# Retention and two expert layers: the first loads, the gate weights and the place of the early ranks rearranged

## The chip, the cores and the metric

The kernel runs on one core of a Trainium2 chip. The metric is the device time of one execution in microseconds; three executions of the kernel before were timed. A core has five engines with a queue of instructions each: TensorE (PE) multiplies matrices, VectorE (DVE), ScalarE (ACT) and GpSimd (POOL) work on tiles, and SyncE (SP) issues transfers (DMA). ACT and POOL issue some transfers too.

## The reference, cut to what matters

Three layers follow each other. q, k and v are (2, 8, 768, 64): two batches, eight heads, 768 tokens, 64 columns.

```python
Dmask = np.where(rel >= 0, lam[:, None, None] ** rel[None, :, :], 0.0)
...
intra = np.einsum('bhic,bhjc->bhij', qb, kb) * Dmask[None]
intra = np.einsum('bhij,bhjd->bhid', intra, vb)
inter = np.einsum('bhid,bhde->bhie', qb * lam_pow[None], kv_state)
...
kv_state = lam_block[None, :, None, None] * kv_state + np.einsum('bhsd,bhse->bhde', kb_dec, vb)
```

That is the retention. Its output, 1536 tokens of 512 columns, goes through a first layer of 8 experts, two for each token, chosen by logits with noise:

```python
logits = x @ w_gate
noise_scale = np.log1p(np.exp(x @ w_noise))
noisy_logits = logits + noise_scale * noise
top2 = np.argpartition(-noisy_logits, 2, axis=1)[:, :2]
...
h = np.maximum(x[mask] @ w1[e], 0.0)
out[mask] += top2_w[mask, k, None] * (h @ w2[e])
```

A second layer of 8 experts takes one expert for each token (`np.argmax(logits, axis=1)`) and has gate weights of its own.

## The kernel before, in words

The retention runs over 12 tiles of 128 tokens, j = 0 to 11, six for each batch. A tile has these pieces on PE, with the copies that other engines make behind them:

- `front(j)`: the transposes of k (L599, four products into the bank `hp`, which ACT copies to `kT` at L601), and for every second tile those of q for two tiles at once (L576, ACT copies to `qT` at L579). The rows of q come from memory with two tokens in turn; `q_rows` sorts them by a copy to `qp` (L558 and L563) ahead of the transposes. L584 makes `qd`, q times the powers of lam.
- `scores(j)` (L632): eight products of k and q into two banks `tr`; DVE multiplies each bank by the mask `dm` to `at` (`masked`, L637).
- `rows(j - 1)` (L700): the products of the tile before with `iw`, a tile that holds the gate weights of the first layer and its noise weights, an identity, and the gate weights of the second layer. DVE takes the logits (L711, L712) and ACT the rows (L709).
- `mix(j)`: the products of `qd` with the state (L679) and of v with `at` (L688), copied by ACT to `xT` (L692), then `state(j)` (L657, bank `yp3`), which DVE adds to the state `st` (L664).

Products of fp32 operands take two passes, so that a product which the program names once stands twice in the trace. The tile framework orders the instructions by their priority and by explicit edges (`tc.issue_after`, here mostly through `behind("name")`, which holds a piece behind the last instruction that `turn` has under that name); each engine then goes through its queue in that order.

At the start nothing can be done before the first loads. SP's queue issues them in the order lam, k of tile 0, two halves of q of tiles 0 and 1, v of tile 0, k of tile 1, q of tiles 2 and 3, v of tile 1, and then the gate and noise weights straight into `iw` and, later, the noise to `nz`: each of these is cut in runs of 32 bytes, because 8 neighbouring numbers belong to one partition. Meanwhile PE multiplies zeros (`unread`, L179): two such products, then the product that spreads lam over the partitions (L185), then five more, and three more between the transposes of k and those of q. Their results are not read.

Among the tiles, expert weights are fetched (`fetch`, tiles `wst`, on SP's queue) in turns that a table of j sets, and rounded by ACT (L108). The first expert is given its tokens early, from the first nine tiles. At j = TA = 9 DVE works out which tokens chose it (`first_marked`, `mbA`); at j = 10 PE counts them (`ranks_of`, L319 and L322, nine products into the bank `yp3`, which `state(9)` used before), DVE turns the counts into numbers `cA` (L763), marks slots with them (`marks`, L381), PE multiplies the marks with the token numbers (`one_hot`, L403), DVE copies the result (L405, `tabi`), PE turns it (L408), DVE makes indices (L409 to L413, `Asrc`) and POOL gathers the rows with them (L530, tiles `xg`). The transposes of these rows (L884) are the last of the retention's part on PE; behind them come the experts (L920 to L922).

## Time and profile before

| | |
|---|---|
| three runs | 594.77, 597.16, 597.49 us; median 597.16 us |
| profiled execution | 595.33 us, of which 593.7 us are the span of the trace |
| PE busy | 583.0 us, 98% of the span |
| DVE, ACT, POOL busy | 375.9, 279.4 and 182.5 us |
| clock of PE, mean over the span | 0.998 of full speed |

The rows further down come from this one profiled execution. A row of the timeline has the start and length of a run of equal instructions in microseconds, counted from the start of the span, then engine, line, operation, out<-in, shapes, and the number of instructions; in brackets stands how long the engine was idle before it and what released it.

### The profile page before, as it was taken

To read this page: it belongs to the slowest core of one execution; us is meant where nothing else is said; L and a number is where in the kernel's file an instruction comes from. 1 tells how busy PE (TensorE), PEld (TensorE's weight loads), DVE (VectorE), ACT (ScalarE), POOL (GpSimd) and SP (SyncE) were. 2 spreads that over 40 slices of the span, in tenths; PEclk is the share of its full clock that TensorE was granted. 3 is DMA by queue.
4 is the path that set the end of the run, shared out by engine and by line. 5 is a ranking of instruction groups with operands and counts; after the bars stand their busy time and mean duration, and the time that the engine had idled before them with its cause. 6 is when DMAs were issued, how large, how long until landed. Compare 5 with 4: busy or idle time off the path is not lost. (4 is left out here: it accounts for less than half of the span.)

```text
span 593.7 us, 11601 instructions
## 1 busy us (share of the span) xinstructions
PE 583.0 (98%) x4305; PEld 554.5 (93%) x4305; DVE 375.9 (63%) x859; ACT 279.4 (47%) x488; POOL 182.5 (31%) x254
## 2 busy tenths in 40 slices
PE   9999999999999999999999999999999999999996
PEld 8988898989999999999999999898889999998996
DVE  5579789765464454543635555447888568667893
ACT  4666431464344433533534434146137367467782
POOL 4976300606041050040220502033175334231204
PEclk9999999999999999999999999999999999999999
DMA  9899505349345377375443621381389967966741
GB/s 183 221 288 279 182 35 195 104 146 357 132 136 172 103 245 224 86 249 177 164 159 106 214 72 54 73 283 69 105 276 340 335 217 236 324 208 198 265 147 36
DMA packets 104868, 109.76 MB, mean 185 GB/s; under 512 B 35699, under 2 KB 80755, under 8 KB 104802
## 3 DMA queue, kind: packets, MB, share of 16 engines
q1 hardware_dynamic: 96722, 83.05, 46.2%
q0 software_dynamic: 8080, 25.88, 12.5%
q8 instruction: 36, 0.59, 0.5%
q14 instruction: 30, 0.25, 0.1%
HBM read 91.89 MB, written 18.71 MB: 186 GB/s over the span
## 5 line engine op out<-in xcount | busy, mean ns | idle before, releaser
L114 DVE TENSOR_TENSOR wl<-wst,wh 128x1024 fp32r<-128x1024 f32 x107 | 133.5, 1256 | 51.9 <-ACT wh L108 49.6
L108 ACT CAST wh<-wst 128x1024 fp32r<-128x1024 f32 x107 | 111.5, 1048 | 35.0 <-PE yp L921 25.3
L920 PE MATMUL hp<-x,wh 128*128 128x364 f32 (+9 forms) x352 | 116.0, 330 | 0.5 <-ACTq L1520 0.5
L921 PE MATMUL hp<-x,wh 128*128 128x364 f32 (+9 forms) x352 | 115.6, 329 | 0.0
L922 PE MATMUL hp<-x,wl 128*128 128x364 f32 (+9 forms) x352 | 114.9, 327 | 0.0
L1008 ACT ACTIVATE h<-hp 128x364 fp32r<-128x364 f32 (+9 forms) x88 | 41.2, 468 | 154.3 <-PE hp L922 147.5
L922 PE MATMUL yp<-h,wl 128*128 128x364 f32 (+8 forms) x320 | 105.9, 331 | 0.0
L920 PE MATMUL yp<-h,wh 128*128 128x364 f32 (+8 forms) x320 | 105.6, 332 | 0.0
L921 PE MATMUL yp<-h,wh 128*128 128x364 f32 (+8 forms) x320 | 105.4, 330 | 0.2 <-DVE h L1009 0.2
L1009 DVE SCALAR_TENSOR_TENSOR h<-hp,h 128x364 fp32r<-128x364 f32 (+9 forms) x88 | 46.3, 526 | 59.5 <-ACT h L1008 59.1
L1167 POOL DMA_INDIRECT x<-y,Rdst x25 | 24.7, 988 | 176.8 <-DVE y L1141 174.7
L920 PEld LDWEIGHTS hp<-x,wh 128*128 128x128 f32 x352 | 66.1, 188 | 1.5 <-ACTq L1520 0.8
L921 PEld LDWEIGHTS hp<-x,wh 128*128 128x128 f32 x352 | 66.1, 188 | 0.5
L922 PEld LDWEIGHTS hp<-x,wl 128*128 128x128 f32 x352 | 66.1, 188 | 0.0
L921 PEld LDWEIGHTS yp<-h,wh 128*128 128x128 f32 x320 | 60.3, 188 | 1.0 <-DVE h L1009 0.6
L922 PEld LDWEIGHTS yp<-h,wl 128*128 128x128 f32 x320 | 60.3, 188 | 0.0
L920 PEld LDWEIGHTS yp<-h,wh 128*128 128x128 f32 x320 | 59.9, 188 | 0.0
L912 DVE TENSOR_TENSOR x<-tr,x 128x128 fp32r<-128x128 f32 (+11 forms) x68 | 27.3, 434 | 26.3 <-ACT x L911 25.7
L911 ACT CAST x<-tr 128x128 fp32r<-128x128 f32 (+11 forms) x68 | 24.4, 386 | 33.4 <-PE tr L910 32.8
L541 POOL TENSOR_TENSOR xg<-xg 128x512 f32<-128x512 f32 (+1 forms) x16 | 24.0, 1502 | 42.6 <-DMA xg<-x,Tsrc 27.8
L530 POOL DMA_INDIRECT xg<-x,Rsrc x25 | 28.7, 1150 | 18.9 <-DVE slt L500 11.6
L1132 PE MATMUL tr<-iw,yT 128*128 128x136 f32 (+3 forms) x224 | 34.2, 287 | 0.1
(393 smaller groups left out, 1041.7 us busy)
## 6 DMA issues: line engine op xcount, KB each, us to landing
wst<-in_moe_w_dram SPq DMA_DIRECT2D x107, 512.0 KB, 4.9
more<-in_moe_w_dram SPq DMA_DIRECT2D x21, 512.0 KB, 5.3
ldk<-in_k_dram SPq DMA_DIRECT2D x12, 256.0 KB, 5.4
ldv<-in_v_dram SPq DMA_DIRECT2D x12, 256.0 KB, 5.8
out_dram<-zero SPq DMA_DIRECT2D x12, 256.0 KB, 4.9
x<-xr SPq DMA_DIRECT2D x11, 256.0 KB, 4.8
ldq<-in_q_dram SPq DMA_DIRECT2D x5, 512.0 KB, 5.8
ldq<-in_q_dram SPq DMA_DIRECT2D x2, 256.0 KB, 4.0
```

The lines of the kernel that those rows point to most:

```text
L108: tail["cast"] = nc.scalar.copy(hi, st).ins
L114: tail["low"] = nc.vector.tensor_sub(lo, st, hi.bitcast(F32)).ins
L530: i = nc.gpsimd.indirect_dma_start(out=r, out_offset=None, in_=x, in_offset=bass.IndirectOffsetOnAxis(ap=src(s)[:m], axis=0))
L911: a = nc.scalar.copy(hi[:, d, :n], ps[:, :n])
L912: v_ = nc.vector.tensor_sub(lo[:, d, :n], ps[:, :n], hi[:, d, :n].bitcast(F32))
L920: nc.tensor.matmul(ps, a[0], b[0], start=start, stop=False)
L921: nc.tensor.matmul(ps, a[0], b[1], start=False, stop=False)
L922: tail["pe"] = nc.tensor.matmul(ps, a[1], b[0], start=False, stop=stop).ins
L1008: tail["act"] = nc.scalar.activation(hh, ps, AF.Relu).ins
L1009: tail["dve"] = nc.vector.scalar_tensor_tensor(hl, ps, 0.0, hh.bitcast(F32), op0=OP.max, op1=OP.subtract).ins
L1132: nc.tensor.matmul(ps[:m, i, :], self.yT[:, 2 * b + i, s * r:s * r + m], iw[:, 2 * b + i, gates2], start=True, stop=True)
L1167: i = nc.gpsimd.indirect_dma_start(out=target, out_offset=bass.IndirectOffsetOnAxis(ap=dst, axis=0), in_=y, in_offset=None, bounds_check=t ...
```

## The change

The first loads come in another order and shape. lam goes to ACT's queue. q of tiles 0 and 1 is loaded as two tiles in its natural order, 256 KB each, so its sorting copies go; `first_front_q` transposes four blocks of it per tile and makes one copy. SP's order is now k, q, v of tile 0, then k, q, v of tile 1. Of the products of zeros, 2 + 3 + 1 are left of 2 + 5 + 3. The gate weights, noise weights and noise are loaded as 24 rows of 4 KB (`load_whole`) on ACT's queue behind the copy of q; eight transposes on PE (`gate_weights`, L230 in the new file) turn them behind `mix(0)`, and four copies on DVE bring them to `iw` and `nz`. Each fetch of expert weights at j = 2 to 6 moves to j = 1 to 5. At j = 10 the ranks stand between the two halves of the scores, both masks stand behind the marks, the product with the marks stands ahead of `front_k(11)`, and the second half of `qd` (L854 on DVE before) is made by POOL. The diff, cut (left out: the new place of a q load in `load`, names that edges refer to, and two edges that put a copy behind another):

```diff
-        parts = (slice(0, HP), slice(HP, H)) if not j else (slice(0, H),)
-        return [lambda h=h: nc.sync.dma_start(t[:, h].rearrange("p h r d -> p h (r d)"), a[:, h]) for h in parts]
+        nc.sync.dma_start(t.rearrange("p h r d -> p h (r d)"), a)
+
+    def first_q():
+        t = ldp.tile([P, H, 2, D], F32, name="ldq", bufs=2).rearrange("p h r d -> p (h r d)")
+        for j in range(2):
+            qkv["q", j] = t[:, j * H * D:(j + 1) * H * D].rearrange("p (h d) -> p h d", h=H)
+        return [lambda j=j: nc.sync.dma_start(qkv["q", j], q[0, :, j * P:(j + 1) * P, :].rearrange("h p d -> p h d"))
+                for j in range(2)]
...
-    i = nc.sync.dma_start(lam1, lam.rearrange("(o h) -> o h", o=1))
+    i = nc.scalar.dma_start(lam1, lam.rearrange("(o h) -> o h", o=1))
+    whole = rt.tile([P, 2, ROW], F32, name="xg", bufs=4).rearrange("p a b -> p (a b)")[:3 * DC + NT, :P * E]
     with tc.issue_after(i.ins):
-        rows_of("k", k, 0)
-        for part in load_q(0):
-            part()
-        written = rows_of("v", v, 0).ins
+        nc.scalar.preload_act_table_set("natural_log_exp_and_others")
+    rows_of("k", k, 0)
+    q_parts = first_q()
+    q_parts[0]()
+    rows_of("v", v, 0)
+    rows_of("k", k, 1)
+    q_parts[1]()
+    written = rows_of("v", v, 1).ins
...
-        unread(5)
+        unread(3)
...
-    with tc.issue_after(written):
-        rows_of("k", k, 1)
-        load_q(2)[0]()
-        rows_of("v", v, 1)
-        nc.sync.dma_start(iw[:, :, :E], g1.rearrange("(c p) e -> p c e", p=P))
-        nc.sync.dma_start(iw[:, :, E:G], gn.rearrange("(c p) e -> p c e", p=P))
...
+    def load_whole():
+        for g, src in enumerate((g1, gn, g2)):
+            nc.scalar.dma_start(whole[g * DC:(g + 1) * DC], src.rearrange("(c p) e -> c (p e)", p=P))
+        nc.scalar.dma_start(whole[3 * DC:], noise.rearrange("(t p) e -> t (p e)", p=P))
+
+    def gate_weights():
+        ps = bank("yp2", [P, E, 3 * DC + NT])
+        n = 3 * DC + NT
+        for e in range(E):
+            turn["state"] = nc.tensor.transpose(ps[:, e, :], whole.rearrange("t (p e) -> t e p", e=E)[:, e, :],
+                                                ident[:n, :n]).ins
+        with tc.issue_after(turn["at"]):
+            for g, a in enumerate((0, E, G + P)):
+                nc.vector.tensor_copy(iw[:, :, a:a + E], ps[:, :, g * DC:(g + 1) * DC].rearrange("p e c -> p c e"))
+            nc.vector.tensor_copy(nz, ps[:, :, 3 * DC:].rearrange("p e t -> p t e"))
...
+    def first_front_q(j):
+        if not j:
+            QT[0] = aw.tile([P, HP, 2, P], F32, name="qT")
+            QD[0] = aw.tile([P, HP, 2, P], F32, name="qd")
+        ps = bank("hp", [P, HP, P])
+        for hp in range(HP):
+            turn["front"] = nc.tensor.transpose(ps[:, hp, :], pair(qkv["q", j], hp), ident).ins
+        turn["copied"] = nc.scalar.copy(QT[0][:, :, j, :], ps).ins
         if j:
-            t = qkv["q", j + 1] = aw.tile([P, 2, H, D], F32, name="qp", bufs=1)
-            with behind("xT", "copied"):
-                nc.scalar.copy(t.rearrange("p r h d -> p h r d"), qkv["q", j])
-            return
-        t = qkv["q", 1] = aw.tile([P, 2, H, D], F32, name="qp", bufs=1)
-        for x, hs in ((nc.scalar.copy, slice(0, HP)), (nc.vector.tensor_copy, slice(HP, H))):
-            with tc.issue_after(decays):
-                i = x(t[:, :, hs].rearrange("p r h d -> p h r d"), qkv["q", 0][:, hs])
-        with tc.issue_after(i.ins):
-            powers_of_q()
+            nc.gpsimd.tensor_mul(QD[0][:, :, 1, :], QT[0][:, :, 1, :], pq)
+
+    def apart(i):
+        tc.add_manual_dep(i.ins, turn["marked"].name, mybir.DependencyInfo(
+            mybir.DependencyClass.Sync, mybir.DependencyReason.DATA), reason="behind the marks")
+        turn["pool"] = i.ins
...
+            with tc.issue_after(decays):
+                powers_of_q()
+        with behind("rows" if j > 1 else "front"):
+            if j < 2:
+                first_front_q(j)
+            elif j % 2 == 0:
+                front_q(j)
+        if not j:
+            with behind("copied"):
+                load_whole()
             with behind("front"):
-                unread(3)
-            q_rows(0)
-        with behind("rows" if j > 1 else "state" if j else "front"):
-            if j % 2 == 0:
-                front_q(j)
+                unread(1)
...
+            if hp == 2 and j == TA + 1:
+                with tc.high_priority(offset=300), tc.issue_after(i.ins):
+                    first_ranked(s1, "yp3")
+                    turn["marked"] = marks(ohA, cA, EARLY[0], range(T0, TA))
+                turn["state"] = tail["ranks"]
             for s in range(2):
                 r = slice(s * D, s * D + D)
                 with behind("state"):
                     i = nc.tensor.matmul(ps[s][:, hp, :], KT[j][r, hp, :], qt[r, hp, j % 2, :], start=True, stop=True)
         turn["scores"] = i.ins
-
-        def masked(s):
-            AT[j, s] = aw.tile([P, HP, P], F32, name="at", bufs=3)
-            turn["at"] = nc.vector.tensor_mul(AT[j, s], ps[s], dm[:, s::2, :]).ins
-
-        masked(0)
+        with behind("marked") if j == TA + 1 else ExitStack():
+            for s in range(2):
+                AT[j, s] = aw.tile([P, HP, P], F32, name="at", bufs=3)
+                turn["at"] = nc.vector.tensor_mul(AT[j, s], ps[s], dm[:, s::2, :]).ins
         if j == TA + 1:
-            with tc.high_priority(offset=300), behind("scores"):
-                first_ranked(s1, "yp3")
-                i = marks(ohA, cA, EARLY[0], range(T0, TA))
-            with tc.issue_after(i):
-                masked(1)
-        else:
-            masked(1)
+            apart(nc.gpsimd.tensor_mul(QD[j - j % 2][:, :, 1, :], QT[j - j % 2][:, :, 1, :], pq))
...
-                if j == 0:
-                    nc.sync.dma_start(iw[:, :, G + P:], g2.rearrange("(c p) e -> p c e", p=P))
-                    nc.sync.dma_start(nz, noise.rearrange("(t p) e -> p t e", p=P))
...
+        if j == TA + 1:
+            with tc.high_priority(offset=300), behind("rows"):
+                selA = one_hot("A", cA, aux1, *EARLY, True, "yp3", oh=ohA)
+                gA = gather(selA[0], EARLY[0], EARLY[0] // EARLY[1], x1[:TA * P, :])
+                turn["picked"] = selA[-1]
+            turn["rows"] = turn["chosen"]
         if not j:
             turn["state"] = turn["scores"]
             state(0)
             front(1)
             mix(j)
+            with behind("state"):
+                gate_weights()
         elif j + 1 < NT:
             front(j + 1)
-        if j == TA + 1:
-            with tc.high_priority(offset=300), behind("front"):
-                selA = one_hot("A", cA, aux1, *EARLY, True, "yp3", oh=ohA)
-                gA = gather(selA[0], EARLY[0], EARLY[0] // EARLY[1], x1[:TA * P, :])
-                turn["picked"] = selA[-1]
-            with tc.high_priority(offset=200), behind("line"):
-                nc.vector.tensor_mul(QD[j - j % 2][:, :, 1, :], QT[j - j % 2][:, :, 1, :], pq)
...
-                for _ in range({2: 1, 3: 1, 4: 1, 5: 1, 6: 1, 9: 1, 10: 2}.get(j, 0)):
+                for _ in range({1: 1, 2: 1, 3: 1, 4: 1, 5: 1, 9: 1, 10: 2}.get(j, 0)):
```

The instructions at the places that this moves stand as follows. First comes PE's queue from its start: `yp` with a number is the bank that takes a product, `zero` the tile of zeros, `xg` the tile with lam (and, in the new kernel, the one with the whole gate weights). Before:

```order
L179 MATMUL yp_118<-zero 128x128 x2
L185 MATMUL yp_121<-xg 128x8
L179 MATMUL yp_124<-zero 128x128 x5
L599 MATMUL hp<-iw,ldk 128x128 x4
L179 MATMUL yp_199<-zero 128x128 x3
L576 MATMUL hp<-iw,qp 128x128 x8
L632 MATMUL tr<-qT,kT 128x128 x8
L657 MATMUL yp_248<-ldv,kd 64x64 x8
L599 MATMUL hp<-iw,ldk 128x128 x4
L688 MATMUL yp_269<-at,ldv 64x128 x8
L632 MATMUL tr<-qT,kT 128x128 x8
```

The same stretch in the changed kernel:

```order
L191 MATMUL yp_123<-zero 128x128 x2
L197 MATMUL yp_126<-xg 128x8
L191 MATMUL yp_129<-zero 128x128 x3
L626 MATMUL hp<-iw,ldk 128x128 x4
L588 MATMUL hp<-iw,ldq 128x128 x4
L191 MATMUL yp_212<-zero 128x128
L670 MATMUL tr<-qT,kT 128x128 x8
L687 MATMUL yp_234<-ldv,kd 64x64 x8
L626 MATMUL hp<-iw,ldk 128x128 x4
L588 MATMUL hp<-iw,ldq 128x128 x4
L719 MATMUL yp_262<-at,ldv 64x128 x8
L230 MATMUL yp_273<-iw,xg 128x24 x8
```

The transposes of q have been split, four ahead of the first scores and four behind the second k, and eight products of 24 columns stand ahead of the second scores, which follow as the next row. ACT's queue from its start, before:

```order
L153 ACT_TABLE_LOAD
L563 COPY qp<-ldq 128x4x2x64
L601 COPY kT<-hp 128x512
L579 COPY qT<-hp 128x512 x2
L601 COPY kT<-hp 128x512
L692 COPY xT<-yp_269 128x512
```

And in the changed kernel:

```order
L164 DMA xg<-in_lam_dram 1x8
L167 ACT_TABLE_LOAD
L628 COPY kT<-hp 128x512
L589 COPY qT<-hp 128x4x128
L223 DMA xg<-in_moe_w_gate_dram 4x1024
L223 DMA xg<-in_moe_w_noise_dram 4x1024
L223 DMA xg<-in_moe_w_gate_dram 4x1024
L224 DMA xg<-in_moe_noise_dram 12x1024
L628 COPY kT<-hp 128x512
L589 COPY qT<-hp 128x4x128
L723 COPY xT<-yp_262 128x512
```

Five issues of transfers have come into ACT's queue, four of them between the first copy of q and the copies for tile 1. DVE's queue at j = 10, from the sum of `state(9)` to the copy of the transposed choice, before:

```order
L664 TENSOR_TENSOR st_172<-st_172,yp_1108 64x4x64 x2
L637 TENSOR_TENSOR at<-tr,dm 128x512
L763 SCALAR_TENSOR_TENSOR cA<-yp_1133,mbA 128x4
L765 TENSOR_SCALAR doneA<-yp_1133 128x1
L381 TENSOR_SCALAR oh<-slot_152,cA 128x288 x4
L637 TENSOR_TENSOR at<-tr,dm 128x512
L711 TENSOR_REDUCE lgs<-yp_1154 128x16
L711 TENSOR_REDUCE lt<-yp_1159 128x16
L712 TENSOR_TENSOR lgs<-lgs,lt 128x16
L405 COPY tabi<-yp_1179 2x288
L854 TENSOR_TENSOR qd<-qT,pq 128x4x128
L409 COPY Aoa<-yp_1190 96x3x2
```

And in the changed kernel:

```order
L694 TENSOR_TENSOR st_167<-st_167,yp_1114 64x4x64 x2
L796 SCALAR_TENSOR_TENSOR cA<-yp_1133,mbA 128x4
L798 TENSOR_SCALAR doneA<-yp_1133 128x1
L403 TENSOR_SCALAR oh<-slot_147,cA 128x288 x4
L675 TENSOR_TENSOR at<-tr,dm 128x512 x2
L743 TENSOR_REDUCE lgs<-yp_1161 128x16
L743 TENSOR_REDUCE lt<-yp_1166 128x16
L745 TENSOR_TENSOR lgs<-lgs,lt 128x16
L428 COPY tabi<-yp_1179 2x288
L432 COPY Aoa<-yp_1190 96x3x2
```

Both masks now stand behind the marks, and the product for `qd` is gone from this queue. On PE, three of the four products of state and `qd` (L679) stood ahead of L408 before; in the changed kernel one does.

## Rows read from the trace of the kernel before

**Rows 1.** The page: busy us, share of the span and instructions of each engine.

```profile
PE 583.0 (98%) x4305; PEld 554.5 (93%) x4305; DVE 375.9 (63%) x859; ACT 279.4 (47%) x488; POOL 182.5 (31%) x254
```

**Rows 2.** Waits of PE, 8 to 76 us: us in total, times, longest us.

```profile
PE tr L884 <- DMA xg<-x,Asrc: 0.7, 1, 0.7
PE yp L700 <- ACT xT L692: 0.4, 1, 0.4
PE hp L599 <- DMA ldk<-in_k_dram: 0.4, 1, 0.4
```

**Rows 3.** Timeline of PE, 1 to 14 us.

```profile
1.19 1.22 PE L179 MATMUL yp<-zero 128*128 128x128 f32 x4 [1.19 <-POOL zero L169]
2.35 0.59 PE L185 MATMUL yp<-xg 1*128 1x8 f32 x2
2.87 2.50 PE L179 MATMUL yp<-zero 128*128 128x128 f32 x10
5.16 1.06 PE L599 MATMUL hp<-iw,ldk 128*128 128x128 f32 x4
...
7.30 1.11 PE L576 MATMUL hp<-iw,qp 128*128 128x128 f32 x8
8.65 1.20 PE L632 MATMUL tr<-qT,kT 64*128 64x128 f32 x16 [0.24 <-ACT qT L579]
...
10.40 0.66 PE L599 MATMUL hp<-iw,ldk 128*128 128x128 f32 x4
...
12.24 1.16 PE L632 MATMUL tr<-qT,kT 64*128 64x128 f32 x16
```

**Rows 4.** Timeline of SP's queue, 0.9 to 5 us, and of ACT, 7 to 9.5 us.

```profile
0.94 0.36 SPq L157 DMA_DIRECT2D xg<-in_lam_dram  x1
1.36 0.41 SPq L134 DMA_DIRECT2D ldk<-in_k_dram  x1
...
2.98 0.51 SPq L134 DMA_DIRECT2D ldv<-in_v_dram  x1
3.53 0.99 SPq L134 DMA_DIRECT2D ldk<-in_k_dram  x1
...
8.01 1.07 ACT L579 COPY qT<-hp 128x512 f32<-128x512 f32 x2 [1.16 <-PE hp L576]
```

**Rows 5.** Transfers issued near 1.4, 3, 3.6 and 9 us: KB, us to landing.

```profile
ldk<-in_k_dram SPq DMA_DIRECT2D x1, 256.0 KB, 3.3
...
ldv<-in_v_dram SPq DMA_DIRECT2D x1, 256.0 KB, 4.9
...
ldk<-in_k_dram SPq DMA_DIRECT2D x1, 256.0 KB, 5.4
...
iw<-in_moe_w_noise_dram SPq DMA_DIRECT2D x1, 16.0 KB, 4.3
```

**Rows 6.** Timeline of DVE, PE and POOL, 62 to 76 us.

```profile
62.80 0.85 DVE L664 TENSOR_TENSOR st<-st,yp 64x256 f32<-64x256 f32 x2
63.71 0.18 PE L319 MATMUL yp<-mbA,tri 128*128 128x5 bf16 x1
64.61 1.46 DVE L381 TENSOR_SCALAR oh<-slot,cA 128x288 bf16<-128x288 f16 x4
65.98 0.68 DVE L637 TENSOR_TENSOR at<-tr,dm 128x512 f32<-128x512 f32 x1
66.77 0.94 PE L679 MATMUL yp<-qd,st 128*128 128x128 f32 x6
66.98 0.44 DVE L405 COPY tabi<-yp 2x288 f32<-2x288 f32 x1
68.83 1.16 POOL L530 DMA_INDIRECT xg<-x,Asrc  x1 [3.47 <-DVE Asrc L413]
70.96 1.29 DVE L637 TENSOR_TENSOR at<-tr,dm 128x512 f32<-128x512 f32 x2 [0.15 <-PE tr L632]
```

**Rows 7.** Timeline of ACT, 33 to 37 us.

```profile
34.32 1.05 ACT L108 CAST wh<-wst 128x1024 fp32r<-128x1024 f32 x1 [1.61 <-DMA wst<-in_moe_w_dram]
```

More of the change, by code (lines that the diff above doesn't have):

```diff
@@ L321, in ranks_of @@
             o = max(0, t + 1 - sl.start)
[L322 to L323 removed]
+            tail["ranks"] = nc.tensor.matmul(ps[:, o:, :], ones, mb[:, t:t + 1, :].to_broadcast([P, n + 1 - o, e]),
+                                             start=False, stop=(t == sl.stop - 1)).ins
         return ps
@@ L585, in half @@
                     if "marked" in turn:
-                        tc.add_manual_dep(i.ins, turn["marked"].name, mybir.DependencyInfo(
-                            mybir.DependencyClass.Sync, mybir.DependencyReason.DATA), reason="behind the marks")
+                        apart(i)
         half(0)
-        if j:
-            turn["half"] = lambda: half(1)
-        else:
-            half(1)
+        turn["half"] = lambda: half(1)
     def front_k(j):
@@ L669, in state @@
             if c + 1 < NC - 1:
-                turn["pool"] = nc.gpsimd.tensor_mul(st[c % 2], new, dec.to_broadcast([P, HP, P])).ins
+                with behind("pool") if "marked" in turn else ExitStack():
+                    turn["pool"] = nc.gpsimd.tensor_mul(st[c % 2], new, dec.to_broadcast([P, HP, P])).ins
     def mix(j):
```

18 lines of the change are left out of this document (11 added, 7 removed).

## The prediction, made before the changed kernel ran

> **What bounds the kernel now.** First the page's table of engines: TensorE (PE) is busy for 98% of the span [rows 1], so time can only be won where PE waits or does work that nobody needs. Next, the waits of PE in the stretch that the change touches, 8 to 76 us: three count, 0.7 us for the last gathered rows, 0.4 us for a copy of ScalarE (ACT), 0.4 us for a load of k [rows 2]. From 76 us on PE runs one expert after the other, and the diff touches nothing there: what the first 76 us gain or lose moves everything behind them, and nothing else does. Then the timeline from the start. The reader is to see two things in it. Four products of 128 columns take 1.06 us at 5.16 and 0.66 us at 10.40, and eight from 7.30 on take 1.11 us [rows 3]: until about 7.4 us PE runs at the lower of its two levels (1.2 GHz), after that at 2.4 GHz, and it had worked almost without a gap since 1.19 us [rows 3] when the clock rose. And the scores of tile 0 start at 8.65 right behind two copies of ACT [rows 3, 4]: the start is a chain of load, transposes, copy. Last the timeline from 62 to 76 us, where the early choice of tokens is made, from the ranks (L319) by marks (L381), product and copy (L405) to the gather (L530) for which PE waits at its end [rows 2, 6].
>
> **The start.** lam leaves SP's queue, so k's first load is issued at 0.94 and not at 1.36 [rows 4] and lands 0.42 us earlier. It landed at 1.36 + 3.3 = 4.66 [rows 4, 5], so now at about 4.24. The loads behind it are q, v, k, q, v, of 256 KB each. v of tile 0 landed at 2.98 + 4.9 = 7.9 and the k behind it at 3.53 + 5.4 = 8.9 [rows 4, 5], a step of 1.05 us for 256 KB. So q lands at 5.3, v at 6.35, k of tile 1 at 7.4, its q at 8.45, its v at 9.5. The rows of q need no sorting copy any more: four transposes at the low clock (1.06) end at 6.4, one copy on ACT (two half ones took 1.07 [rows 4]; I take 0.6) ends at 7.0, and the scores start at about 7.1, 1.55 us before the old 8.65. The products of zeros that go (four of ten) stood only in front of these waits and win nothing themselves.
>
> Then the gain is given back. From scores 0 to scores 1 it took 12.24 - 8.65 = 3.59 us [rows 3]. Into this stretch come four transposes of tile 1's q, of which the pitch is 0.11 (1.11 for eight behind each other [rows 3], with the tail), so 0.45, and eight transposes of the gate weights with 24 columns each. These have no row; from below they cost nothing, from above the 1.11 of eight with 128 columns; I take 0.6, and 0.15 for one more change of operands. Without a wait scores 1 would start at 7.1 + 3.6 + 0.45 + 0.75 = 11.9, 0.35 us earlier than before.
>
> But they wait for the noise, and that is the last of four loads that ACT issues. By the order of its waits it takes the semaphore of tile 1's v, so ACT stands still until that v has landed at 9.5. Behind it on ACT's queue stand the copies of k and q of tile 1 (ready at about 10.8 to 11.4 then, early enough for scores 1). How long the noise takes from 9.55 on is the disputed price. From below: lam, four bytes a head and with nothing else under way, went from its issue at 0.94 to the product at 2.35 that read it [rows 3, 4], 1.4 us. From above: the 16 KB of noise weights took 4.3 us behind the big loads in SP's queue [rows 5]. I take 2.2, nearer to lam, because the new loads are 24 runs of 4 KB on a queue of their own, where the old ones were 3072 runs of 32 bytes. Landed at 11.75; PE would have been there at 7.1 + 3.6 + 0.45 = 11.15. So PE waits 0.6 us and scores 1 start at 12.5, **0.25 us later** than before; by the lower bound 0.35 earlier, by the upper one 2.35 later. The four copies to the tiles that hold weights and noise lie on VectorE (DVE) under scores 1 (1.16 us [rows 3]) and cost nothing; without that cover some 0.7 us.
>
> The Trainium skill bears on that price: DMA: Bandwidth & Descriptors, section "Queues, rings and completion order", says that each DMA engine takes turns between the queues it has work for, packet by packet. By it a load on ACT's queue does not stand behind SP's backlog, and the start would come out 0.35 us earlier instead of 0.25 later. No row of before has two queues of loads at work, so the trace neither shows nor denies it; it is the first rival.
>
> **The loop between.** Every fetch of expert weights moves one turn forward (j = 1 to 5 instead of 2 to 6), and the 3072 short runs are gone from in front of k and v. ACT waited 1.61 us for a weight tile before its cast at 34.32 [rows 7], the copy behind it came late, and PE waited the 0.4 us. The k load that PE missed by 0.4 us stood behind weights in the queue. With an earlier fetch and a freer queue both waits should go: **-0.8**, at worst 0 (one fetch more now stands ahead of that k: 512 KB, by the step above 2.1 us, against the gains just named). What is late next is the gather.
>
> **The ranks inside the scores.** At j = 10 the ranks stand between the halves of the scores. They need the bank that state 9 has just left, and DVE reads that bank until 62.80 + 0.85 = 63.65; the ranks already started right there, at 63.71 [rows 6]. So they cannot come earlier; the second half of the scores, which PE did meanwhile, comes behind them: 0.6 later, half of the 1.16 that scores take [rows 3]. On DVE both masks now follow the marks, which end at 64.61 + 1.46 = 66.07. Two masks take 1.29 (row at 70.96), and from the end of the one mask (65.98 + 0.68) to L405 at 66.98 it took another 0.32 for three small ones [rows 6]. So L405 starts at 66.07 + 1.29 + 0.32 = 67.7 instead of 66.98, or at 67.6 with the overlap that follows from their pitch: 0.6 later, and L408 and the gather behind it with it. QD's product (L854) goes from DVE to GpSimd (POOL) and lies there ahead of the gather; POOL had been idle for 3.47 us before it [rows 6], so it costs nothing; without that gap it would cost at least the 0.68 that DVE takes for a mask of that size [rows 6]. On PE two of the L679 products that stood ahead of L408 (six passes in 0.94) now stand behind it, four passes of 0.11, so PE comes to the gathered rows 0.6 + 0.45 = 1.05 late. It waited 0.7 for them. Gather 0.6 late: **+0.6**; were the rows there in time, 1.05 - 0.7 = +0.35; and were the wait of 0.7 a thing of this one execution, +1.05.
>
> **Sum.** +0.25 - 0.8 + 0.6 = +0.05 us on the profiled execution's 595.33 (span 593.7 and 1.63 around it): 595.4. The median of the three runs is 597.16, 1.8 us above the profiled one, and the runs lie 2.7 apart, about 0.5%; less than that a measurement of this kernel can hardly tell from no change. On the median I say **597.2**.
>
> **Rivals.** *The loads of ACT pass the backlog* and the gather comes in time: -0.35 - 0.8 + 0.35 = -0.8, so 596.4. For it: small runs, own queue. Against: ACT itself is held until 9.5. Chance 0.25. *The same with more:* the queue so relieved that waits too small for the list of waits go too. From scores 1 on PE's row has small gaps only, so I allow 2 us more, 594.4 or below; chance 0.1. *The clock rises later*, the one on the slower side. Fewer products of zeros leave PE idle ahead of k at 4.2, ahead of q at 5.2, ahead of the scores at 6.9 and ahead of the gate weights, where before it worked without a gap up to the rise at 7.4. A microsecond more at the low level costs half a microsecond of work (1.06 against 0.66 and less [rows 3]). If it rises only behind the gate weights, near 13, that is (13 - 7.4) / 2 = 2.8 us, so 600.0; it decides against the forecast from a rise near 9 on. The Trainium skill speaks for this rival: TensorE: Matmul & The Clock Gate, Part 1, has the throttled state as the default, which activity releases. Chance 0.2. *The change does nothing at j = 10:* the ranks wait for DVE anyway, which is counted above.
>
> **How the numbers follow.** Forecast 0.45, loads that pass 0.25, much relieved queue 0.1, late clock 0.2. The first two lie between 596.4 and 597.5 and, with the bounds of the noise (-0.6 to +2.1) and of the gather (-0.25 to +0.45) and the scatter of the runs, between 595 and 599. The range reaches to both others: 594.3 to 600.0. Faster by over 0.5% (below 594.2) only in a part of the relieved queue: 0.1. Slower by over 0.5% (above 600.1) in the worse part of the late clock and with a noise that lands as late as the upper bound: 0.1. Same: 0.8.
>
> **What the profile after would show.** The first scores near 7.1 and PE idle ahead of the transposes with 24 columns, released by a DMA: right on the start; no idle time there and scores 1 before 12: the first rival. Groups of four at 1.06 us behind 7.5 us: the late clock. No wait for wst or ldk in ACT's and PE's rows: right on the loop. The ranks released by DVE's sum, L405's successor 0.6 us later against the ranks, and PE still waiting for the gather: right at j = 10. The forecast is wrong if the stretch up to the first expert product has become more than 3 us longer or shorter, or if PE loses or wins behind it.

## The result: 1% slower, and the profile after

The changed kernel takes 602.38 us (median of 6 runs, 601.49 to 603.51), the kernel before 596.77 us (6 runs, 594.77 to 597.49): 1.0096 times as long, 95% interval 1.0077 to 1.0116. Forecast was 597.2 us, with a range up to 600.0, and a chance of 0.1 for slower by over 0.5%. The profiled execution took 602.59 us with a span of 601.0 us, against 593.7 before.

First the table of engines on the page of the changed kernel, and PE's waits from 8 to 85 us (us in total, times, longest):

```profile
PE 587.7 (98%) x4305; PEld 558.2 (93%) x4305; DVE 372.9 (62%) x861; ACT 278.8 (46%) x487; POOL 184.6 (31%) x254
```

```profile
PE yp L230 <- DMA xg<-in_moe_noise_dram: 3.0, 1, 3.0
PE yp L341 <- DVE st L694: 0.4, 1, 0.4
PE yp L719 <- DVE at L675: 0.2, 1, 0.2
```

PE's share is the same as in [rows 1], but it is busy 4.7 us longer with equally many instructions: some of its work has become slower. The three waits of [rows 2] are gone, and one new wait is longer than the three together. The timeline of PE shows both, and answers to [rows 3]:

```profile
2.87 1.65 PE L191 MATMUL yp<-zero 128*128 128x128 f32 x6
4.35 1.09 PE L626 MATMUL hp<-iw,ldk 128*128 128x128 f32 x4
5.44 1.11 PE L588 MATMUL hp<-iw,ldq 128*128 128x128 f32 x4
...
7.23 2.08 PE L670 MATMUL tr<-qT,kT 64*128 64x128 f32 x16 [0.25 <-ACT qT L589]
...
10.29 1.12 PE L626 MATMUL hp<-iw,ldk 128*128 128x128 f32 x4
11.20 0.86 PE L588 MATMUL hp<-iw,ldq 128*128 128x128 f32 x4
11.99 1.09 PE L719 MATMUL yp<-at,ldv 128*64 128x128 f32 x16
16.10 1.04 PE L230 MATMUL yp<-iw,xg 24*128 24x24 f32 x8 [3.01 <-DMA xg<-in_moe_noise_dram]
17.07 2.08 PE L670 MATMUL tr<-qT,kT 64*128 64x128 f32 x16
19.08 2.29 PE L731 MATMUL yp<-iw,xT 128*128 128x144 f32 x8
...
25.34 1.16 PE L670 MATMUL tr<-qT,kT 64*128 64x128 f32 x16
```

The last row is the scores of tile 2. In the kernel before it stood at 18.20:

```profile
18.20 1.16 PE L632 MATMUL tr<-qT,kT 64*128 64x128 f32 x16
```

The reader is to see the same pieces with two lengths. Scores (L670) take 2.08 us at 7.23 and at 17.07 and took 1.16 to 1.20 before; L719 at 11.99 takes 1.09, the length at the upper level. By the record of the granted clock it rises to 2.4 GHz at 11.73 (before: 7.44), falls to 1.2 GHz at 15.14, 2.1 us into the wait for the noise (13.09 to 16.10), and rises again at 21.97. Two stretches of the changed kernel in one view (us, then busy us and instructions of PE, PEld, DVE, ACT and POOL, the clock, the DMA share and GB/s):

```profile
11.73:15.14 3.41, 1.36 (x19) 0.94 (x17) 0.00 (x0) 2.52 (x4) 3.11 (x8) 1.00 1.28 236
15.14:21.97 6.83, 5.87 (x36) 5.62 (x37) 2.20 (x8) 0.74 (x2) 1.77 (x8) 0.50 1.05 238
```

PE works 5.87 us at half speed in the second one. The queue of ACT, 6 to 13 us, says why the noise is late, and the rows of SP's queue stand below it:

```profile
6.59 0.58 ACT L589 COPY qT<-hp 128x512 f32<-128x512 f32 x1 [0.53 <-PE hp L588]
6.60 0.25 ACTq L223 DMA_DIRECT2D xg<-in_moe_w_gate_dram  x1
6.89 0.31 ACTq L223 DMA_DIRECT2D xg<-in_moe_w_noise_dram  x1
8.03 0.26 ACTq L223 DMA_DIRECT2D xg<-in_moe_w_gate_dram  x1
10.52 0.30 ACTq L224 DMA_DIRECT2D xg<-in_moe_noise_dram  x1
11.45 0.58 ACT L628 COPY kT<-hp 128x512 f32<-128x512 f32 x1 [4.27 <-PE hp L626]
```

```profile
5.12 1.33 SPq L134 DMA_DIRECT2D ldv<-in_v_dram  x1
6.50 1.15 SPq L134 DMA_DIRECT2D ldk<-in_k_dram  x1
7.68 1.14 SPq L143 DMA_DIRECT2D ldq<-in_q_dram  x1
8.87 1.23 SPq L134 DMA_DIRECT2D ldv<-in_v_dram  x1
10.28 1.69 SPq L134 DMA_DIRECT2D ldk<-in_k_dram  x1
```

The noise is issued at 10.52, when v of tile 1 (issued at 5.12) has landed at 10.50: ACT held it back until then, because both loads use one semaphore. By its semaphore the noise lands at 15.96, 5.4 us behind its issue, and PE goes on at 16.10. Of these 5.4 us, 2.9 pass before its first packet moves (13.42), 1.4 while its 48 KB move (to 14.82) and 1.1 from there to the semaphore. Ahead of it SP had issued k, q and v of tile 2 (256, 512 and 256 KB). With the loads of tiles 0 and 1 that makes 2560 KB, and 2478 KB of SP's queue had moved at 13.42. The first loads of gate weights show the same: issued from 6.60 on, when SP had issued the 1536 KB of tiles 0 and 1, they begin to move at 9.20, when SP's queue has moved 1527 KB.

Measured from scores to scores in the two profiles, the loss sits in one place. Scores of tile 2 start at 25.34 instead of 18.20: **+7.1**. From there to scores of tile 10 it takes 43.0 instead of 44.4: **-1.4**. From scores 10 (68.34; 62.62 before) to the first expert product (83.98; 76.89 before) 15.6 instead of 14.3: **+1.4**. From there to the end of PE's last product it takes 512.3 instead of 511.8 us, 0.5 more, which is within what this part varies from run to run (510.6 to 512.4 us in the profiles in which the clock did not fall there), and what follows PE's last product takes 0.3 less. The spans differ by 7.3 us, the medians by 5.6.

### The profile page after: what moved, and what is told of

It is laid out like the page before. It is cut to its first block, busy times and chain, and to the rows that moved or that the text cites. A ratio compares the mean times of both kernels' runs of the same rounds, so it can differ in the third digit from the quotient of the medians.

```text
span 601.0 us, 11607 instructions
## 1 busy us (share of the span) xinstructions
PE 587.7 (98%) x4305; PEld 558.2 (93%) x4305; DVE 372.9 (62%) x861; ACT 278.8 (46%) x487; POOL 184.6 (31%) x254
## 3 DMA queue, kind: packets, MB, share of 16 engines
HBM read 91.89 MB, written 18.71 MB: 184 GB/s over the span
## 5 line engine op out<-in xcount | busy, mean ns | idle before, releaser
L114 DVE TENSOR_TENSOR wl<-wst,wh 128x1024 fp32r<-128x1024 f32 x107 | 135.3, 1273 | 52.0 <-ACT wh L108 47.7
```

The lines of the kernel that those rows point to most:

```text
L114: tail["low"] = nc.vector.tensor_sub(lo, st, hi.bitcast(F32)).ins
```

## The experiments

Theory N: the late noise is the loss, by its wait and by the clock that falls in it. Theory C: the products of zeros that were taken away are the loss, since they make the clock rise late. Theory J: the new order at j = 10 costs what the profile pair shows. The table has for every run, in the order of this section, when the granted clock rose (and where it fell again within the first 85 us), when the scores of tiles 1 and 2 started, how long it took from scores 2 to 10, from scores 10 to 11 and from there to the first expert product (all from its profile, us), and the ratio to the kernel before on the same chip.

| run | clock rises | scores 1 | scores 2 | 2 to 10 | 10 to 11 | to expert | ratio, 95% |
|---|---|---|---|---|---|---|---|
| before | 7.44 | 12.24 | 18.20 | 44.42 | 7.15 | 7.12 | |
| changed | 11.73, low again 15.14 to 21.97 | 17.07 | 25.34 | 43.00 | 8.04 | 7.60 | 1.0096 [1.0077, 1.0116] |
| e1 zeros back | 5.47, low again 15.71 to 22.54 | 16.93 | 25.55 | 43.00 | 8.04 | 7.64 | 1.0112 [1.0073, 1.0151] |
| e2 loads early | 11.57 | 14.24 | 20.20 | 43.00 | 8.03 | 7.60 | 1.0030 [1.0016, 1.0044] |
| e3 old gate loads | 8.93 | 11.75 | 18.56 | 44.71 | 8.03 | 7.58 | 1.0017 [0.9999, 1.0035] |
| e4 early and zeros | 4.95 | 12.70 | 18.84 | 43.68 | 8.03 | 7.60 | 1.0016 [0.9995, 1.0037] |
| e5 old j = 10 | 5.66 | 12.69 | 18.71 | 43.59 | 7.15 | 7.16 | 0.9991 [0.9979, 1.0002] |
| e6 j = 10 alone | 7.49 | 12.27 | 18.23 | 43.20 | 8.03 | 6.56 | 1.0007 [0.9993, 1.0021] |
| e7 old fetches | 5.60 | 12.85 | 19.35 | 43.32 | 8.03 | 6.55 | 0.9997 [0.9983, 1.0012] |
| e8 ranks behind | 6.32 | 12.69 | 18.89 | 43.03 | 7.11 | 6.60 | 0.9986 [0.9968, 1.0004] |
| e9 before, fewer zeros | 12.48 | 13.58 | 19.54 | 43.02 | 7.16 | 8.06 | 1.0013 [0.9994, 1.0033] |
| e10 noise apart | 6.10, low again 12.93 to 19.76 and 30.0 to 33.4 | 13.34 | 22.35 | 46.70 | 8.04 | 7.60 | 1.0065 [1.0044, 1.0085] |
| e11 before, mild j = 10 | 7.62, low again 48.6 to 52.0 | 12.33 | 18.29 | 46.93 | 7.12 | 7.80 | 1.0025 [1.0009, 1.0042] |
| e12 new start, old gates | 7.14 | 11.53 | 18.50 | 44.81 | 7.12 | 7.80 | 1.0033 [1.0021, 1.0046] |
| e13 noise ahead of k2 | 6.22, low again 19.87 to 23.29 | 12.38 | 22.28 | 43.45 | 8.04 | 6.55 | 1.0041 [1.0026, 1.0057] |
| e14 e11, old fetches | 5.89 | 11.87 | 17.99 | 44.64 | 7.12 | 6.55 | 0.9987 [0.9973, 1.0001] |
| e15 e8 again | 7.99 | 12.96 | 18.92 | 43.58 | 7.11 | 6.56 | 0.9998 [0.9987, 1.0009] |

Runs e1 to e4 shared one chip, e5 to e8 a second, e9 to e12 a third; e13 to e15 were on the second again. For the pair, before and changed, the record names no chip. Each row but the ratio is one profiled execution. In those of e2 and e3 (600.92 and 600.52 us, 3.7 and 3.9 above their medians) the clock fell once more near 445 us, among the experts; the ratios go by all runs.

### Noise or zeros: e1 to e4

**e1**, the products of zeros as before:

```diff
-        unread(3)
+        unread(5)
...
-                unread(1)
+                unread(3)
```

> The change, with the products of zeros as before (2, 5 and 3). Theory N (the late noise): the noise lands near 16 us whatever PE does before, so PE only reaches the gate weights sooner and waits longer; the clock rises near 7.5 us but falls again in that wait; scores of tile 1 near 17, time 602.4, as with the whole change (within 0.7). Theory C (the missing products of zeros make the clock late, and that is the loss): the clock rises near 7.5 and stays, and the time comes back by 3 us or more, to 599.5 or below.

**e2**, the four loads right behind lam:

```diff
+    for g, src in enumerate((g1, gn, g2)):
+        i = nc.scalar.dma_start(whole[g * DC:(g + 1) * DC], src.rearrange("(c p) e -> c (p e)", p=P))
     with tc.issue_after(i.ins):
         nc.scalar.preload_act_table_set("natural_log_exp_and_others")
+    with tc.issue_after(i.ins):
+        nc.scalar.dma_start(whole[3 * DC:], noise.rearrange("(t p) e -> t (p e)", p=P))
...
-            with behind("copied"):
-                load_whole()
```

> The change, with the four loads of gate weights and noise issued on ACT's queue right behind lam, ahead of the table load (the noise behind lam's landing), so that they stand behind almost nothing. Theory N: no wait at the gate weights, no second low stretch of the clock (the 6.8 us at 15.14 to 21.97 go); scores of tile 1 near 14 instead of 17.07; time 602.4 - 3.0 - 2.9 = 596.5 (595.5 to 598). Theory C: the clock still rises late and the loss stays except for the wait itself: 599 to 600.

**e3**, the loads of gate weights and noise as before:

```diff
-            with behind("copied"):
-                load_whole()
...
-            with behind("state"):
-                gate_weights()
...
+        nc.sync.dma_start(iw[:, :, :E], g1.rearrange("(c p) e -> p c e", p=P))
+        nc.sync.dma_start(iw[:, :, E:G], gn.rearrange("(c p) e -> p c e", p=P))
...
+                    nc.sync.dma_start(iw[:, :, G + P:], g2.rearrange("(c p) e -> p c e", p=P))
+                    nc.sync.dma_start(nz, noise.rearrange("(t p) e -> p t e", p=P))
```

> The change without the whole loads and without the eight transposes: gate weights and noise go to their tiles as before, in short runs on SP's queue, everything else as changed. Theory N: no wait for a load between mix of tile 0 and scores of tile 1, no second low stretch; scores of tile 1 near 13; time 596 to 598. Theory C: clock rises as late as with the change and may fall, 599 to 600.

**e4** is e2 with the diff of e1.

> Early loads and the products of zeros as before, both together. Theory N with the late first rise as a second, smaller term: the clock rises near 7.5 instead of 11.7, some 2 us less than with the early loads alone, scores of tile 1 near 12.3, time 594.5 to 595.5. Theory C: as with the zeros alone less the wait, 596.5.

PE's timeline in e1, in e2 and in e4, from scores 0 to scores 1:

```profile
7.08 1.16 PE L670 MATMUL tr<-qT,kT 64*128 64x128 f32 x16
...
15.96 1.05 PE L230 MATMUL yp<-iw,xg 24*128 24x24 f32 x8 [5.05 <-DMA xg<-in_moe_noise_dram]
16.93 2.08 PE L670 MATMUL tr<-qT,kT 64*128 64x128 f32 x16
```

```profile
7.84 2.08 PE L667 MATMUL tr<-qT,kT 64*128 64x128 f32 x16 [0.25 <-ACT qT L588]
...
13.25 1.06 PE L229 MATMUL yp<-iw,xg 24*128 24x24 f32 x8
14.24 1.16 PE L667 MATMUL tr<-qT,kT 64*128 64x128 f32 x16
```

```profile
7.57 1.16 PE L667 MATMUL tr<-qT,kT 64*128 64x128 f32 x16
...
11.72 1.05 PE L229 MATMUL yp<-iw,xg 24*128 24x24 f32 x8
12.70 1.16 PE L667 MATMUL tr<-qT,kT 64*128 64x128 f32 x16
```

With the zeros alone the clock rises at 5.47 and scores 0 run at full speed, but PE only waits longer, 5.05 us instead of 3.01, falls to the low level in the wait, and starts scores 1 at the low level at 16.93. Nothing is won (1.0112): Theory C is refuted as the cause of the loss. With the loads early there is no wait and no fall, although the clock rises as late as in the changed kernel (11.57): scores 2 come 5.1 us earlier, and the ratio goes from 1.0096 to 1.0030. Theory N is shown, with one correction that e10 brings below. Once the wait is gone the late rise is a price of its own: with the zeros back (e4) scores 2 come another 1.36 us earlier, and the median on the same chip goes from 597.27 to 595.91. e3 removes the wait as well; the time that its shorter way to scores 1 (11.75) wins goes at tile 8, see below.

### The order at j = 10 and the fetches: e5 to e8

**e5** is e4 with everything of the change at j = 10 undone: `scores`, the place of `one_hot` and the product for `qd`.

> Early loads and old products of zeros (the fourth run), and the stretch at j = 10 as before: ranks behind the whole scores, one mask ahead of the marks, half of qd on DVE, product with the marks behind front_k. Theory J (the new order at j = 10 costs 1.36 us, 15.63 instead of 14.27 us from scores 10 to the first expert product): that stretch returns to 14.3 and the time to 595.9 - 1.4 = 594.5 (593.8 to 595.3). Rival (the stretch is longer because of what the start and the fetches did to the transfers): stays near 15.6, time 595.9.

**e6** is the kernel before with these same hunks of the change and nothing else.

> The kernel before with the new order at j = 10 alone. Theory J: scores 10 to first expert product 15.6 instead of 14.3, time 1.4 us over before. By the prediction's own term: 0.6 over before, with PE still waiting for the gathered rows. Rival: no change.

**e7** is e4 with one line back:

```diff
-                for _ in range({1: 1, 2: 1, 3: 1, 4: 1, 5: 1, 9: 1, 10: 2}.get(j, 0)):
+                for _ in range({2: 1, 3: 1, 4: 1, 5: 1, 6: 1, 9: 1, 10: 2}.get(j, 0)):
```

> Early loads and old products of zeros (the fourth run), and the table of fetches as before (turns 2 to 6). If the earlier turn is what took the waits between scores 2 and scores 10 away (44.4 us before, 43.0 with the change): the stretch grows to 44.4 and ACT waits for a weight tile again; time 596.5. If it was the short runs that left SP's queue: 43.0 to 43.7, time 595.9.

**e8** is e4 with `scores` as before, except for two lines that keep the product on POOL:

```diff
                 first_ranked(s1, "yp3")
-                i = marks(ohA, cA, EARLY[0], range(T0, TA))
+                turn["marked"] = i = marks(ohA, cA, EARLY[0], range(T0, TA))
             with tc.issue_after(i):
                 masked(1)
+            apart(nc.gpsimd.tensor_mul(QD[j - j % 2][:, :, 1, :], QT[j - j % 2][:, :, 1, :], pq))
```

> Early loads and old products of zeros (the fourth run), with the ranks behind the whole scores and one mask ahead of the marks again, but half of qd on POOL and the product with the marks ahead of front_k as changed. If the place of ranks and masks is the loss at j = 10: the stretch returns to 14.3 to 14.7, time 594.7. If the place of the product or of qd is: it stays above 15.2, time 595.6 or more.

The stretch from scores 10 to the first expert product is 14.31 in e5, 14.59 and 14.58 in e6 and e7, 13.71 in e8. Theory J holds in sign and not in size: the new order costs 0.3 us here, not 1.36. It has two parts that nearly cancel. Ranks between the halves of the scores cost 0.9 (8.03 against 7.11 to 7.16 from scores 10 to 11, in every run that has them). Product ahead of `front_k` and `qd` on POOL win 0.6 (6.55 to 6.60 against 7.12 to 7.16): PE no longer waits for the gathered rows. e8 has the gain without the loss, and its ratio is the lowest, but its interval still holds 1.

e6 tells another thing. Its loads and fetches are those of the kernel before, and from scores 2 to 10 it takes 43.20, as e9 does with 43.02, where the profiled execution of before took 44.42; e7, with the old fetches behind the new start, takes 43.32. But e14 below, again with the loads and fetches of before, takes 44.64, and e8 and its repetition e15, which are one kernel on one chip, take 43.03 and 43.58. So the waits behind the 1.4 us that the change seemed to win come in some executions of the old order and not in others, and one pair of profiles can't price them. What the earlier fetches win in every profile is small: the step from scores 6 to 7 takes 4.19 to 4.24 us in all twelve profiles with them and 4.22 to 4.64 in the five others.

### Zeros by themselves, noise by itself, and two attempts at a faster kernel: e9 to e12

**e9**: the kernel before with 3 instead of 5 and 1 instead of 3 in `unread`.

> The kernel before with 2, 3 and 1 products of zeros instead of 2, 5 and 3, nothing else. If the products of zeros set when the clock rises: it rises later than 7.4 us (9 to 12), scores 1 come 0.7 to 2 us later, time 0.1 to 0.3% above before. If they do not: rise near 7.4, time as before.

**e10**: the noise has a tile and transposes of its own, behind `mix(2)`:

```diff
+    def gate_noise():
+        ps = bank("yp3", [P, E, NT])
+        for e in range(E):
+            turn["state"] = nc.tensor.transpose(ps[:, e, :], apart_n.rearrange("t (p e) -> t e p", e=E)[:, e, :],
+                                                ident[:NT, :NT]).ins
+        nc.vector.tensor_copy(nz, ps.rearrange("p e t -> p t e"))
...
+        if j == 2:
+            with behind("state"):
+                gate_noise()
```

> The change, with the noise turned by eight products of its own behind mix of tile 2 and the gate weights alone turned behind mix of tile 0. Theory N (it is the noise, the last of the four loads, that PE waits for): no wait at the gate weights, which landed at 12.5 in the changed kernel, no fall of the clock; scores of tile 1 near 14.2, and 0.9 us more for the eight products at tile 2; time 0.3 to 0.5% above before, where the whole change has 0.96%. Rival (any product that needs the whole loads waits as long): wait of 2 us or more, time 0.8% or more above.

**e11**: the kernel before with the hunks of e8 and the new table of fetches.

> The kernel before with three parts of the change: half of qd on POOL, the product with the marks ahead of front_k at j = 10 (ranks behind the whole scores as before), and fetches one turn earlier. From the eighth run: scores 10 to first expert product 13.7 instead of 14.3, time 0.6 to 0.8 us below before. Rival (these gains need the new start): as before.

**e12**: e8 with the loads of e3.

> As the eighth run (new start, products of zeros as before, ranks behind the whole scores), with gate weights and noise loaded as before in short runs on SP's queue and no transposes of them. If the eight transposes are what the new start gives back: scores of tile 1 near 11.6 instead of 12.7, time 1 us below the eighth run, 0.25% below before. If the short runs on SP's queue hold the next k and q: scores of tile 2 at 18.5 or later, time as the eighth run or worse.

e9, PE from 2.8 us on:

```profile
2.87 1.65 PE L179 MATMUL yp<-zero 128*128 128x128 f32 x6
4.56 1.09 PE L599 MATMUL hp<-iw,ldk 128*128 128x128 f32 x4
...
8.47 2.08 PE L632 MATMUL tr<-qT,kT 64*128 64x128 f32 x16
...
13.58 1.16 PE L632 MATMUL tr<-qT,kT 64*128 64x128 f32 x16
```

The products of zeros bear on the rise: in e9 it comes at 12.48 instead of 7.44, and scores 1 come 1.34 us later. The time is 0.13% above before, which the interval does not separate from none. Over all profiles the rise lies at 4.95 to 7.99 in the eleven with 2, 5 and 3 products, and at 6.10 to 12.48 in the six with 2, 3 and 1, so fewer zeros allow a late rise and do not force it.

e10 did not come out as expected. The gate weights alone came late too: PE waited 1.5 us for them (10.91 to 12.38), since the clock had risen at 6.10 and PE was there sooner, and the clock fell behind that shorter wait as well (12.93 to 19.76). So it is not the noise as such, but any of these loads that PE needs before it has landed. The products for the noise at tile 2 came behind another gap of 1.1 us on PE, and the clock fell once more (30.0 to 33.4); both falls are in its 46.70.

e11 and e12 were to be faster than before and came out slower (1.0025 and 1.0033). They lost at tile 8 what they should have won. In e12 the start did what was asked, with scores 1 at 11.53, but 6.97 us passed from there to scores 2, so that these come only 0.39 earlier than in e8. PE's waits from 44 to 56 us, in e11 and in e12:

```profile
PE hp L604 <- DMA ldk<-in_k_dram: 1.2, 1, 1.2
```

```profile
PE hp L612 <- DMA ldk<-in_k_dram: 1.4, 1, 1.4
```

The three kernels that have the short runs of gate weights on SP's queue and the earlier fetches together (e3, e11, e12) wait 1.2 to 1.5 us for k of tile 8. None of the thirteen others waits there longer than the kernel before; e14, which is e11 without the earlier fetches, has no such wait, and takes 6.39 us from scores 7 to 8 where e11 takes 9.84. In e11 the clock fell in this wait (48.6 to 52.0). In e3 and e12 it did not, though they waited no less: scores 8 ran in 1.16 us there.

### The load of the noise, and what belongs to the chip: e13 to e15

What was open: whether a load that ACT issues stands behind what SP issued before it, or takes 5 us in itself; and whether the late sum of DVE at j = 11 (below) belongs to the change. **e13** holds SP's loads of tile 2, and all behind them, until the noise has landed (cut; in it ACT also issues the noise without a wait for v of tile 1):

```diff
+        if (n, j) == ("k", 2):
+            tc.add_manual_dep(i.ins, turn["noise"].name, mybir.DependencyInfo(
+                mybir.DependencyClass.Sync, mybir.DependencyReason.DATA), reason="behind the noise")
```

> The change, with the loads of k, q and v of tile 2 and all behind them on SP's queue held until the noise has landed; the noise is issued behind the first copy of q, near 7.5 us, without waiting for v of tile 1. If a load of ACT stands behind what SP issued before it (in the changed kernel the noise, issued at 10.52, landed at 15.96 between v of tile 2 at 15.40 and k of tile 3 at 17.0): it lands with or right behind v of tile 1, at 10.5 to 11.5, no wait of PE, no fall of the clock, scores of tile 1 near 14.2, time 0.3% above before. Rival (a load of ACT takes some 5 us whatever is ahead): it lands near 13, and PE still waits a little.

**e14** is e11 with the old table of fetches.

> The kernel before with half of qd on POOL and the product with the marks ahead of front_k at j = 10, nothing else (the eleventh run without the earlier fetches). If the wait for k of tile 8 in the eleventh run came from the earlier fetches: no such wait, step from scores 7 to 8 near 6.1, time 0.1% below before (0.05 to 0.2%). Rival (that wait came from the chip): wait again, time as the eleventh run, 0.25% above.

**e15** is e8 unchanged.

> The kernel of the eighth run once more, on whatever chip this is. DVE's sum of state 10 was 0.1 us late behind its products in all four runs of that call and 0.7 to 1.6 us late in the calls before and after, with either order at j = 10. If that lateness belongs to the chip: it shows in all three runs of this call or in none. If it belongs to the code: it stays at 0.1 here and may differ in the others. Time 0.13% below before, as then, or 0.1% above if the sum is late.

e13: ACT's issue of the noise, SP's first issue that waits for it, and PE at the gate weights:

```profile
7.45 0.30 ACTq L229 DMA_DIRECT2D xg<-in_moe_noise_dram  x1
```

```profile
11.07 0.37 SPq L134 DMA_DIRECT2D ldk<-in_k_dram  x1
```

```profile
11.39 1.06 PE L235 MATMUL yp<-iw,xg 24*128 24x24 f32 x8
12.38 1.16 PE L675 MATMUL tr<-qT,kT 64*128 64x128 f32 x16
...
18.65 1.09 PE L612 MATMUL hp<-iw,qp 128*128 128x128 f32 x8 [1.88 <-ACT qp L585]
```

The noise landed by 11.07, 3.6 us after its issue and 0.8 after v of tile 1 (10.27 by its semaphore). PE did not wait at the gate weights. The packets of the two queues show the order: q1 is SP's, q10 ACT's (packets, MB, share of 16 engines); first 7.45 to 9 us, then 9 to 11.1 us of e13:

```profile
q1 hardware_dynamic: 1335, 0.34, 136.1%
q10 hardware_dynamic: 1, 0.00, 1.1%
```

```profile
q10 hardware_dynamic: 47, 0.09, 19.3%
q1 hardware_dynamic: 135, 0.03, 9.9%
```

ACT's four loads were issued from 6.46 on, and until 9 us only one packet of them moved; the others moved from 9.0 to 10.5, as SP's backlog came to its end (SP issued nothing between 6.15 and 11.07). So they stand behind what SP had issued, as in the changed kernel, where the noise packets run from 13.4 us on. The rival, that a load of ACT takes some 5 us whatever is ahead, does not hold: it took 3.6 us here. The hold itself is no gain: the wait went to q of tile 2 (1.88 us, until 18.65), and the clock fell 1.2 us behind it (19.87 to 23.29).

The late sum: in the changed kernel DVE's sum of state 10 (L694) starts 1.4 us behind the end of the products that it needs (L687), where before it started 0.12 us behind them. The rows of PE, DVE and POOL in the changed kernel (among them POOL's third gather of rows and DVE's masks behind the sum), then of PE and DVE in e13, which has the same code at that place:

```profile
75.81 0.63 PE L687 MATMUL yp<-ldv,kd 128*64 128x64 f32 x16
...
77.68 0.92 POOL L553 DMA_INDIRECT xg<-x,Asrc  x1 [0.30 <-issue]
77.83 0.85 DVE L694 TENSOR_TENSOR st<-st,yp 64x256 f32<-64x256 f32 x2 [3.15 <-PE tr L670]
...
79.26 1.29 DVE L675 TENSOR_TENSOR at<-tr,dm 128x512 f32<-128x512 f32 x2 [0.58 <-PE yp L731]
```

```profile
73.20 0.63 PE L692 MATMUL yp<-ldv,kd 128*64 128x64 f32 x16
73.95 0.85 DVE L699 TENSOR_TENSOR st<-st,yp 64x256 f32<-64x256 f32 x2 [1.88 <-PE yp L692]
```

The sum is late by 0.7 to 1.6 us in all eight profiles of the first and third chip (e9, with the old code, among them) and by 0.1 us in all seven of the second, whichever code they have. So in these fifteen runs it goes with the chip. The change does not make it: e9 has it with the old code, and e13 lacks it with the new. The sum is not alone. The masks behind it start 2.9 to 3.3 us behind scores 11 in the nine late profiles (the changed kernel is the ninth) and 1.2 us behind in the eight others, and PE waits for the sum, the masks or both; the last column of the table is 7.58 to 8.06 with this and 6.55 to 7.16 without. In all nine the masks start 0.64 to 0.69 us behind the end of POOL's third gather (above, 77.68 + 0.92 and 79.26); in the eight others they start before that gather does. That points at the gathers, but no run moved them, and what differs between the chips stays open.

## Why the prediction was wrong

**What bounds the kernel: right.** The first 26 us lose 7.1, and the experts are untouched. The stretch up to the first expert product has become 7.1 us longer, which by the prediction's own sign (more than 3 us) makes it wrong.

**The first scores: right.** Forecast near 7.1, measured 7.23.

**The price of the noise: this step failed.** The prediction took 2.2 us for the landing, "nearer to lam, because the new loads are 24 runs of 4 KB on a queue of their own", with 1.4 and 4.3 as bounds. Measured are 5.4 from the issue at 10.52. The row at the upper bound, 4.3 us behind the big loads [rows 5], was the nearer neighbour, and still too short: e13 shows that a queue of its own does not pass SP's backlog, and in the changed kernel 1 MB of tile 2 stood ahead. A second term was small beside it: v of tile 1 was taken to land at 9.5 and landed at 10.5, as the five loads of 256 KB behind the first took 1.26 us each by their semaphores (4.22 to 10.50) and not 1.05. PE's wait became 3.0 us and not 0.6, although PE itself came to the gate weights only at 13.09 and not at 11.15. A third term was sized without a row: 0.75 for the eight transposes, which take 0.97 (changed) to 0.99 (e13). The four copies on DVE, said to cost some 0.7 without cover, again without a row, took 0.55 and lay under scores 1 as forecast.

**What a wait does to the clock: missing.** The prediction priced a wait by its length alone. In the wait of the changed kernel the clock fell, and PE worked 5.87 us at the low level afterwards: from scores 1 to scores 2 it took 8.27 us instead of 5.96, 2.3 more. With the wait that makes 5.3, close to the 5.1 us that e2 wins back at scores 2. The rivals had the clock as a late rise only.

**The rival of the late clock** came true at its place and not in its price. The rise came at 11.73, but in the changed kernel all of that was hidden in front of the noise, since e1 rises at 5.47 and is no faster. Where nothing waits behind it, it costs 1.36 us (e2 against e4). The rule of the Trainium skill that was named there (TensorE: Matmul & The Clock Gate, Part 1: throttled is the default state) agrees with the fall at 15.14, in a place that the prediction did not apply it to.

**The rival of loads that pass the backlog** (0.25), with the Trainium skill's rule of turns packet by packet beside it, is refuted for loads of ACT behind loads of SP by e13's packets, and with it the rival of a much relieved queue (0.1), which built on it. In that run one packet of ACT's loads moved between 7.45 and 9 us while 1335 of SP's did. The prediction says that no row of before has two queues at work. That holds for its rows, but not for the trace: from 137 to 138 us POOL's queue moved 60 packets of gathered rows beside 150 packets of SP's weights, so POOL's loads do share with SP's there. The same section of the Trainium skill (DMA: Bandwidth & Descriptors, "Queues, rings and completion order") says that the increment of a load's semaphore lands only after every earlier write of its DMA engine, across the queues. That agrees with where the noise landed, 15.96 by its semaphore, between v of tile 2 (15.40) and k of tile 3 (17.0); it does not explain that its packets began only at 13.4.

**The loop: right in the pair of profiles, not shown as a cause.** Forecast -0.8, measured -1.4, and the waits for wst and ldk are gone. But e6 and e9 lack them too, without the earlier fetches or the freer queue, and e14 has the long stretch again (44.64): they come in some executions only, and that the pair agreed with the forecast was partly luck.

**j = 10: right in its steps, off in its size.** The ranks are released by DVE's sum (0.4 us in the list of waits), and from scores 10 to 11 PE loses 0.9, where 1.05 was forecast. "PE still waiting for the gather" was wrong: the rows were there in time, the case that was given +0.35, and e6 and e7 have +0.3. The other 1.1 us of the pair's +1.4 are the late sum and masks, which the change does not cause.

So the terms stand as +0.25, -0.8, +0.6 against +7.1 (4.8 of it at scores 1, where the +0.25 was put), -1.4, +1.4 in the pair of profiles. The medians differ by less than the profiles, 5.6 against 7.3 us: the profiled execution of before (595.33) is 1.4 us below its median, that of the changed kernel (602.59) at its own.

No version beats the kernel before by more than its interval: e8 came to 0.9986 and then to 0.9998, e14 to 0.9987 with an interval up to 1.0001.

## What to carry to other kernels

A load that PE needs early must be issued early: here ACT's queue did not help it past what SP had issued before (5.4 us for 48 KB), and the semaphore that it shared with a large load held ACT from 8.3 to 10.5 us. A wait of PE may have to be priced twice, by its length (3.0 us) and by the work that then runs at half clock (2.3 us more), and work ahead of it (zeros or a faster front) wins nothing until the wait is gone. A wait that one profile of the kernel before shows is a gain only if other executions show it too.

## What the runs showed of the hardware that was not expected

The clock of PE fell in waits of 3.0 us (changed) and 5.05 us (e1) and 0.55 us behind one of 1.5 us (e10), and the low level lasted 6.8 us each time, well into work without a gap. It lasted 3.4 us behind a wait of 1.9 us (e13) and in one of 1.2 us (e11), and in e3 and e12 waits of 1.5 and 1.4 us at tile 8 passed without a fall, so the length of a wait alone does not tell. ACT's 4 KB packets, issued from 6.46 us on, moved only when the loads that SP had issued before them were all but through, near 9 us (e13). DVE's sum at j = 11 started 0.1 us behind PE's products on one chip and 0.7 to 1.6 us behind them on two others, whichever code ran.
